# Dummy matmuls first, early zeroing on VectorE and an unheld w_in load in an attention-then-MLP kernel

## The chip, the cores and the metric

The kernel runs on one core of a Trainium2 chip. The metric is the device time of one execution in microseconds. Times of the kernel before are the median of three runs; the profile is of one further execution on the same core, taken by the hardware profiler.

## The reference

Batch 8, 8 heads, 576 positions, head dimension 64. First comes a Nyström form of attention with 32 landmarks: q and k are averaged over segments of 18 positions, three softmaxes are taken (q with the landmarks of k, landmarks with landmarks, landmarks of q with k), and the middle one is inverted by six Newton steps. The result goes through a two-layer MLP with squared ReLU.

```python
q_lm = q.reshape(B, H, m, S // m, D).mean(axis=3)
k_lm = k.reshape(B, H, m, S // m, D).mean(axis=3)
A = sm(q, k_lm)
Bm = sm(q_lm, k_lm)
C = sm(q_lm, k)
Z = Bm.transpose(0, 1, 3, 2) / (norm1(Bm) * norminf(Bm) + 1e-06)
for _ in range(6):
    Z = 2 * Z - Z @ Bm @ Z
x = A @ Z @ C @ v            # then heads side by side: 4608 x 512
r = np.maximum(x @ w_in, 0.0)
out = (r * r) @ w_out        # w_in 512 x 2048, w_out 2048 x 512
```

## The kernel before, in words

The eight batches are worked through one after the other. For a batch, the attention of batch b + 1 is woven into the MLP of batch b. The attention is folded into the first MLP matrix: instead of x the kernel forms G, a product of the small C times v with w_in, and multiplies it with the transposed rows of A (AT, or AZ with the inverse folded in, for batch 0). Function mlp_in does that for 16 feature tiles of 128 each (line 824), ScalarE takes the ReLU out of PSUM into a tile r (line 828), of which there are three, and VectorE squares it into gT (line 829). Function mlp_out multiplies gT with w_out (line 853).

The order of instructions on TensorE, VectorE, ScalarE and SyncE is written out by hand: the string HEAD holds the order for the attention of batch 0, and PLANS that of each batch after it, as tokens. In HEAD, ck casts k of batch 0 (VectorE one half at line 719, ScalarE the other at 720), tk and tq are TensorE transposes of k and q (line 315), tt those of the tail rows (line 325), mk and mq the segment means (line 344) with their evacuations at 359 and 360, ek, eq and et evacuations of transposes (lines 731 and 736), cq the copies of q (line 725), lm the landmark scores (line 374), ib, if, jo, jl and nu the inversion, and g the product with w_in (line 807). A token w:n:width issues n dummy matmuls of that width on zeros (function warm, line 297, 512 wide where no width is given); their result in the tile idle is never read. In PLANS, pk and pq prepare k and q of the next batch: a VectorE copy into another layout at line 283, from the tile stage for batches 1 and 2. Token h is one feature tile of mlp_in, s one squaring.

What isn't in that hand-written order is issued by a scheduler that goes by readiness: the constants at the start (zeroed tiles bd0, bd1, vt, ect, the segment matrix seg with GpSimd's band selections at line 206, the identity, the mask), and GpSimd's loads. GpSimd issues nearly all loads, one after the other, each held behind the one before by issue_after; k of batch 0 alone goes over the SyncE queue. The loads of batch 0's q come first. Function load_rest then queues the rest in the order of LOADS (two parts of w_in, v of batch 0, k and q of batch 1, two parts of w_in, four of w_out, v of batch 1). The first of these carries a further wait, called gate: it may not start before ScalarE's half of the cast of k is done. After the last of them GpSimd copies one column block of seg into the slot NC4 + 2, which the means of odd batches read at line 354, and zeroes two tiles ct0 and ct1 (line 264), 128 x 1280 bf16 each. These c-value tiles are read only where a batch number reaches DMA_C, which is 9.

```python
DMA_C = 9
        behind[:] = [masked]
        gate[:] = [after]
        for x in LOADS.split():
```

Of the kernel before, what the change touches and what calls it, by code (L numbers as in the profile page):

```python
# [9 lines left out]
P = 128  # L10
# [4 lines left out]
BF16 = mybir.dt.bfloat16  # L15
# [12 lines left out]
NC4 = 4  # L28
# [5 lines left out]
DMA_C = 9  # L34
COMPACT = 1
HEAD = (
    "ck tk1 mk w:1:256 w:1:256 ek1d w:1:256 w:1 tk0 tt w:1 w:1 cq0 cq1 ek0a mq tq0 tq1 lm "
    "w:1 et w:1:256 w:1 eq0a w:1:256 tl eq1d ls sum:0:4:5 w:1 ib w:1 w:1:256 sq1 w:1:256 if "
    "sk1 sum:1:2:5 w:1:256 w:1 sum:1:0:2 jo w:1:256 w:1:256 rec:1 w:1:256 row:1:0:3 "
    "row:1:3:5 w:1:256 sk0 w:1 sq0 jo w:1:256 w:1:256 w:1 w:1:256 sum:0:2:4 sum:0:0:2 w:1 jo "  # L40
    "rec:0 cv:0 cv:1 w:1:256 w:1:256 row:0:3:5 cr jo w:1:256 row:0:0:3 w:1:256 at:1 cba w:1 "
    "jl at:0 ea0d ea1a ct w:1:256 nu w:1:256 g:0 gl1d fv w:1 gf1d w:1 gf0a az gl0d"
# [46 lines left out]
def kernel(  # L89
# [9 lines left out]
    nc = tc.nc  # L99

    const = ctx.enter_context(tc.tile_pool(name="const", bufs=1))
# [19 lines left out]
    vts, ects, cts = [], [], []  # L121
# [8 lines left out]
    behind, gate = [], []  # L130

    def load(dst, src, queue=nc.gpsimd):
        with tc.issue_after(behind[0].ins) if behind else nullcontext():
            d = queue.dma_start(dst, src)  # L134
        if gate:
            tc.add_manual_dep(
                d.ins, gate.pop().ins.name,
                mybir.DependencyInfo(mybir.DependencyClass.Sync, mybir.DependencyReason.DATA),
                reason="q first")
        if queue is nc.gpsimd:  # L140
            behind[:] = [d]
        return d
# [66 lines left out]
    seg = const.tile([P, NC4 + 3, M], BF16, name="seg")  # L209
# [21 lines left out]

    EA = const.tile([P, 2, NC4 + 1, P], F32, name="EA")
    nc.vector.memset(EA[:, :, NC4, :], 1.0)

    def load_rest(after):

        def w_in(i, j):
            load(
                w_in_bf[64 * i:64 * i + 64, :, 1024 * j:1024 * j + 1024],
                moe_w_in[256 * i:256 * i + 256, 1024 * j:1024 * j + 1024].rearrange(  # L240
                    "(j d) f -> d j f", d=D),
            )

        def w_out(j):
            load(
                w_out_bf[:, 4 * j:4 * j + 4, :],
                moe_w_out[512 * j:512 * j + 512, :].rearrange("(ft fp) c -> fp ft c", fp=P),
            )

        behind[:] = [masked]  # L250
        gate[:] = [after]
        for x in LOADS.split():
            i = int(x[1])
            if x[0] == "w":
                w_in(i, int(x[2]))
            elif x[0] == "o":
                w_out(i)
            else:
                (load_v if x[0] == "v" else load_qk)(i, loaded[i])
        with tc.issue_after(behind[0].ins):  # L260
            nc.gpsimd.tensor_copy(seg[:, NC4 + 2, :], seg[:, NC4, :])
            for i in range(2):
                ct = const.tile([P, 2, NC4 + 1, P], BF16, name="ct%d" % i)
                nc.gpsimd.memset(ct[:], 0.0)
                cts.append(ct)

    turn = [0]

# [31 lines left out]
    def attention(b: int, R: dict):  # L300
# [410 lines left out]
        def head_step(token):  # L711
# [5 lines left out]
            if name == "ck":  # L717
                raw = natural(0, "k")
                dve(X["k"][:, 0:2], raw[:, 0:2])
                load_rest(act(X["k"][:, 2:4], raw[:, 2:4]))  # L720
                st["qraw"] = natural(0, "q")
                X["tT"] = attn.tile([P, NPAIR, P], BF16, tag="tT", name="tT")
# [253 lines left out]
```

The softmax here doesn't subtract the row's maximum and nothing guards it: scores larger than these inputs give would overflow.

## Time and profile before

| | us |
|---|---|
| median of three runs | 265.70 |
| the three runs | 265.61, 265.70, 266.66 |
| span of the profiled execution | 264.8 |
| TensorE busy | 248.2 |
| VectorE busy | 176.4 |
| ScalarE busy | 158.5 |
| GpSimd busy | 47.8 |
| first TensorE instruction starts | 8.01 |
| k of batch 0 cast by VectorE and ScalarE from | 6.91 |
| first w_in load issued | 8.25 |
| GpSimd's zeroing of ct0 and ct1 | 27.50, for 2.28 |

A group's line in the page gives the source line, engine, operation, the tile written and the tiles read, their shape and the count, then busy time and mean of one in ns. In the timeline the first two columns are start and length in microseconds, and a bracket holds the idle time of the engine before the instruction and what ended it. In the chain of waits each piece has its start, the time by which it alone moved the chain on, and its engine and line. PE is TensorE, PEld its weight loads, DVE is VectorE, ACT ScalarE and POOL GpSimd.

### The profile page before, as it was taken

What the parts mean: (1) busy time and instruction counts of PE and PEld (TensorE: products, weight loads), DVE (VectorE), ACT (ScalarE), POOL (GpSimd) and SP (SyncE); (2) the same over time, 40 slices, a digit from 0 to 9 for tenths busy, and PEclk for the clock granted to TensorE, in tenths of its full rate; (3) what the DMA queues carried; (4) which work ended last, traced back from release to release, by engine and by line L of the source; (5) the groups of instructions that cost most, each with busy time, mean ns of one, the idle gap of its engine ahead of it and who ended that gap; (6) DMA issues with size and microseconds to landing.
All of it is one profiled execution on the core that took longest, in us unless ns stands there. A gap on an engine that the chain in (4) does not pass through costs nothing.

```text
span 264.8 us, 6918 instructions
## 1 busy us (share of the span) xinstructions
PE 248.2 (94%) x2835; PEld 153.7 (58%) x2878; DVE 176.4 (67%) x485; ACT 158.5 (60%) x278; POOL 47.8 (18%) x73
## 2 busy tenths in 40 slices
PE   0799899999999999999999999999999999999994
PEld 0675665467665656566556565666566655555443
DVE  3488986879985779689766589689776884232100
ACT  1364887279666765678457565674777665365210
POOL 7744623302010500700003201320000000000000
PEclk9999999999999999999999999999999999999999
DMA  8999999998159899996829998999911111112122
GB/s 183 161 190 202 209 205 189 214 208 107 32 101 188 98 197 178 184 203 124 121 74 115 172 192 114 128 191 188 159 42 40 42 40 65 56 40 83 40 79 79
DMA packets 69791, 34.65 MB, mean 131 GB/s; under 512 B 37376, under 2 KB 64256, under 8 KB 69760
## 3 DMA queue, kind: packets, MB, share of 16 engines
q0 software_dynamic: 39808, 17.83, 54.2%
q1 hardware_dynamic: 24704, 7.08, 17.3%
q10 hardware_dynamic: 5248, 9.31, 11.3%
q8 instruction: 22, 0.36, 0.6%
q14 instruction: 9, 0.07, 0.1%
HBM read 36.70 MB, written 9.44 MB: 174 GB/s over the span
## 4 chain that ended last, share of the span: by engine, by line
PE 87%; DVE 5%; DMA 2%; issue 2%; ACT 2%; ACTq 0%
PE ops L853 24%; PE h L824 22%; PE n L853 21%; PE n L532 3%; PE g L807 3%; DMA stage<-in_k_dram 2%; PE idle L297 2%; PE n L416 2%; PE n L344 2%; PE n L598 2%; PE n L616 1%; DVE nat L283 1%; DVE gT L829 1%; PE tps L315 1%; PE n L631 1%
## 5 line engine op out<-in xcount | busy, mean ns | idle before, releaser
L828 ACT ACTIVATE r<-h 128x576 bf16<-128x576 f32 x128 | 81.3, 652 | 46.4 <-PE h L824 35.1
L853 PE MATMUL ops<-w_out_bf,gT 128*128 128x512 bf16 (+1 forms) x300 | 76.8, 368 | 0.9 <-issue 0.3
L853 PEld LDWEIGHTS <-gT 128*128 128x128 bf16 x592 | 53.2, 98 | 38.7 <-issue 4.2
L829 DVE TENSOR_TENSOR gT<-r 128x576 bf16<-128x576 bf16 x128 | 54.9, 448 | 26.3 <-ACT r L828 26.1
L824 PE MATMUL h<-AT,G 128*128 128x288 bf16 x448 | 71.0, 286 | 0.2
L853 PE MATMUL n<-w_out_bf,gT 128*128 128x512 bf16 x252 | 69.7, 379 | 1.1 <-issue 0.3
L824 PEld LDWEIGHTS <-G 128*128 128x128 bf16 x512 | 47.7, 97 | 24.3 <-issue 0.8
L705 DVE CAST G<-g 128x1024 bf16<-128x1024 f32 x14 | 17.1, 1224 | 5.4 <-PE g L807 5.4
L864 ACT COPY o_sb<-ops 128x512 f32<-128x512 f32 (+1 forms) x19 | 10.9, 574 | 14.5 <-PE ops L853 14.5
L864 ACT COPY o_sb<-n 128x512 f32<-128x512 f32 x17 | 10.0, 587 | 12.9 <-PE n L853 12.8
L705 ACT CAST G<-g 128x1024 bf16<-128x1024 f32 x14 | 14.2, 1013 | 4.5 <-PE g L807 4.5
L134 POOL DMA_DIRECT2D raw<-in_k_dram x5 | 4.6, 921 | 53.2 <-DVE gT L829 28.1
L532 PEld LDWEIGHTS <-T 128*128 128x128 bf16 x256 | 11.3, 98 | 4.2 <-issue 0.6
L574 DVE TENSOR_REDUCE ra<-EA 128x20 f32<-128x640 f32 (+3 forms) x19 | 13.2, 704 | 0.3 <-ACT EA L562 0.3
L586 DVE TENSOR_TENSOR an<-EA,rra 128x640 bf16<-128x640 f32 (+2 forms) x18 | 13.2, 736 | 0.2
L532 PE MATMUL n<-bd,T 128*128 128x64 bf16 x256 | 12.7, 193 | 0.3 <-issue 0.2
L315 PEld LDWEIGHTS <-nat 128*128 128x128 bf16 x96 | 6.8, 108 | 9.8 <-ACT nat L720 8.0
L537 ACT ACTIVATE EA<-n 128x512 f32<-128x512 f32 x16 | 9.6, 598 | 3.3 <-PE n L532 3.2
L134 POOL DMA_DIRECT2D raw<-in_q_dram x5 | 4.4, 884 | 38.5 <-DVE rc L447 28.1
L537 ACT ACTIVATE EC<-n 128x512 bf16<-128x512 f32 x16 | 9.5, 596 | 3.0 <-PE n L532 1.6
L315 PE MATMUL tps<-ident_bf,nat 128*128 128x128 bf16 x32 | 3.4, 278 | 8.0 <-ACT nat L720 8.0
L824 PE MATMUL h<-AZ,G 128*128 128x288 bf16 x64 | 10.0, 286 | 0.6 <-DVE AZ L797 0.4
(144 smaller groups left out, 294.6 us busy)
## 6 DMA issues: line engine op xcount, KB each, us to landing
out_dram<-o_sb ACTq DMA_DIRECT2D x31, 256.0 KB, 3.1
vm<-in_v_dram POOLq DMA_DIRECT2D x8, 512.0 KB, 10.1
raw<-in_k_dram POOLq DMA_DIRECT2D x5, 512.0 KB, 6.9
raw<-in_q_dram POOLq DMA_DIRECT2D x5, 512.0 KB, 6.1
w_in_bf<-in_moe_w_in_dram POOLq DMA_DIRECT2D x4, 512.0 KB, 12.1
w_out_bf<-in_moe_w_out_dram POOLq DMA_DIRECT2D x4, 512.0 KB, 17.2
out_dram<-o_sb ACTq DMA_DIRECT2D x9, 128.0 KB, 2.4
stage<-in_k_dram SPq DMA_DIRECT2D x1, 1024.0 KB, 6.1
```

Source lines behind the costliest of these rows:

```text
L134: d = queue.dma_start(dst, src)
L315: nc.tensor.transpose(tps[:, i, p, :], X[nm][:, 2 * half + i, 2 * p:2 * p + 2, :].rearrange("p h d -> p (h d)"), ident_bf[:],)
L532: nc.tensor.matmul(sc[:, c, j, :, :], lhsT=X[nm + "T"][:, c, p, :], rhs=BD[:, 1 if nm == "q" else 0, p, 0:64], start=True, stop=True)
L537: nc.scalar.activation(dst, sc.rearrange("p c j i m -> p c (j i m)"), AF.Exp, scale=SCALE)
L574: nc.vector.reduce_sum(ra[:, quads, lo:hi, :], EA[:, quads, lo:hi, :].rearrange("p q c (h m) -> p q c h m", m=M), axis=AX.X)
L586: on.tensor_tensor(an[:, i, lo:hi, :].rearrange("p c (h m) -> p c h m", m=M), EA[:, i, lo:hi, :].rearrange("p c (h m) -> p c h m", m=M), r ...
L705: (act, dve)[n % 2](G[:, :, n * 512:n * 512 + 512], gg[:])
L824: nc.tensor.matmul(h[:, j, 0:HALF], lhsT=G[:, qd, f * P:(f + 1) * P], rhs=AT[:, qd, a0 + j * HALF:a0 + (j + 1) * HALF], start=(qd == 0), s ...
L828: nc.scalar.activation(r.rearrange("p (j t) -> p j t", j=2), h[:, :, 0:HALF], AF.Relu)
L829: return lambda: nc.vector.tensor_tensor(gT[:, f, o:o + S], r[:], r[:], ALU.mult)
L853: nc.tensor.matmul(ops, lhsT=gT[:, f, t * P:t * P + P], rhs=w_out_bf[:, f, i * n:i * n + n], start=(f == 0), stop=(f == NF - 1))
L864: nc.scalar.copy(o_h, ops)
```

## The change

Three edits at the start of the kernel. HEAD begins with w:16, sixteen dummy matmuls 512 wide, ahead of the cast of k; they are meant to bring TensorE up to its full pace before real work arrives. The copy of the seg block and the zeroing of ct0 and ct1 move from GpSimd, behind its loads, to VectorE, next to the other constants. And the gate is gone: the first w_in load waits only until GpSimd has issued the mask, so that the loads behind it start earlier too.

```diff
 HEAD = (
-    "ck tk1 mk w:1:256 w:1:256 ek1d w:1:256 w:1 tk0 tt w:1 w:1 cq0 cq1 ek0a mq tq0 tq1 lm "
...
+    "w:16 ck tk1 mk w:1:256 w:1:256 ek1d w:1:256 w:1 tk0 tt w:1 w:1 cq0 cq1 ek0a mq tq0 tq1 "
...
     EA = const.tile([P, 2, NC4 + 1, P], F32, name="EA")
     nc.vector.memset(EA[:, :, NC4, :], 1.0)
+    for i in range(2):
+        ct = const.tile([P, 2, NC4 + 1, P], BF16, name="ct%d" % i)
+        nc.vector.memset(ct[:], 0.0)
+        cts.append(ct)
+    nc.vector.tensor_copy(seg[:, NC4 + 2, :], seg[:, NC4, :])
...
         behind[:] = [masked]
-        gate[:] = [after]
         for x in LOADS.split():
...
-        with tc.issue_after(behind[0].ins):
-            nc.gpsimd.tensor_copy(seg[:, NC4 + 2, :], seg[:, NC4, :])
-            for i in range(2):
-                ct = const.tile([P, 2, NC4 + 1, P], BF16, name="ct%d" % i)
-                nc.gpsimd.memset(ct[:], 0.0)
-                cts.append(ct)
```

The remaining lines of HEAD hold the same tokens, broken differently.

## The prediction

> **What bounds the kernel now.** I read the page's busy times, the chain of work that ended last, the timeline, and the traffic in half-microsecond stretches.
>
> ```profile
> PE 248.2 (94%) x2835; PEld 153.7 (58%) x2878; DVE 176.4 (67%) x485; ACT 158.5 (60%) x278; POOL 47.8 (18%) x73
> ```
>
> TensorE is busy 94% of the span, so from about 40 us on only less matmul work would help, and the change removes none there. What is left is the start: nothing runs on TensorE before 8.01 us, and a microsecond saved ahead of the steady part is a microsecond off the end, if nothing else holds the later work back. The chain of waits from 0 to 60 us begins so (start, length, piece):
>
> ```profile
> 0.81 6.08 DMA stage<-in_k_dram
> 6.91 1.05 ACT nat L720
> 8.01 1.03 PE tps L315 x8
> 9.04 0.53 PE n L344 x20
> 9.58 1.07 PE idle L297 x4
> 10.64 0.85 PE tps L315 x8
> 11.50 0.43 PE n L325 x4
> 11.92 0.85 PE idle L297 x2
> 12.78 0.53 PE n L344 x20
> 13.31 1.15 PE tps L315 x16
> ```
>
> The reader should see two things. Until 8.0 us the load of k and ScalarE's cast of it set the time. Then TensorE does, at half pace: two dummies 512 wide take 0.85 us, 0.425 each, and eight transposes take 0.85 to 1.03. Later in the same trace one 512-wide matmul of line 853 takes 0.22 in the chain, and eight transposes 0.45 (at 58.71). The sixteen at 13.31 take 1.15, between the two paces, so the switch came during them, near 13.7. The page's row for the granted clock reads 9 throughout and doesn't show it; the durations do.
>
> The second place is in batch 0's MLP (start, length, engine, line, tiles, and the idle time before with its releaser):
>
> ```profile
> 27.50 2.28 POOL L264 MEMSET ct<- 128x1280 bf16 x2
> 27.80 2.54 DVE L283 COPY nat<-stage 128x2048 bf16<-128x2048 bf16 x1
> 30.39 1.07 PE L315 MATMUL n<-ident_bf,nat 128*128 128x128 bf16 x16 [0.66 <-DVE nat L283]
> 30.79 1.19 ACT L828 ACTIVATE r<-h 128x576 bf16<-128x576 f32 x2 [0.90 <-DVE gT L829]
> ```
>
> The copy of q of batch 1 takes 2.54 us; the same copy of k at 26.21 takes 0.68. It ran beside GpSimd's two zeroings of the c-value tiles and ended 0.56 after them. TensorE and ScalarE then waited 0.66 and 0.90 for VectorE.
>
> The third is the load queue. Over these stretches the last column is GB/s:
>
> ```profile
> 8.50:9.00 0.50, 0.50 (x11) 0.50 (x9) 0.00 (x0) 0.00 (x0) 0.50 (x2) 1.00 1.35 183
> 9.00:9.50 0.50, 0.50 (x22) 0.50 (x20) 0.00 (x0) 0.00 (x0) 0.50 (x1) 1.00 0.47 59
> 9.50:10.00 0.50, 0.50 (x6) 0.31 (x3) 0.36 (x2) 0.32 (x2) 0.50 (x2) 1.00 1.03 61
> 10.00:10.50 0.50, 0.50 (x4) 0.21 (x2) 0.50 (x1) 0.21 (x1) 0.50 (x2) 1.00 0.52 49
> 10.50:11.00 0.50, 0.50 (x7) 0.50 (x6) 0.50 (x3) 0.00 (x0) 0.50 (x1) 1.00 0.84 160
> ```
>
> From 9.0 to 10.75 the loads nearly stop: batch 0's q is through, and the first w_in load was issued at 8.25, after 1.84 us of waiting for ScalarE's cast.
>
> [...]
>
> **The change, part by part.**
>
> *Sixteen dummies 512 wide, first in TensorE's order.* They need only bd1, zeroed by about 1.5. All slow, they take 16 x 0.425 = 6.8 us, to 8.4. [...] They lie beside the load of k; at worst they hold the first transposes by 0.4. Then the pieces above run fast. At half the time, eight transposes go from 1.03 to 0.52 and, at the 0.45 of 58.71, from 0.85 to 0.45, the dummies from 1.07 to 0.53 and 0.85 to 0.43, the tail's four transposes from 0.43 to 0.22, the sixteen from 1.15 to 0.90, the limit of the one row that has sixteen partly fast (at 0.056 each; both ends alike within 0.1). The two means (20 matmuls, 0.53) stay: 32 of them take 0.85 in full pace at 57.03, the same each. Sum before 6.44, after 4.11: 2.3 less. VectorE then has to follow: its evacuation (L360) at 9.06, the T copy until 10.08, the two casts of q (0.81) until 10.85, 0.2 after TensorE could take them. That leaves 2.1 in the profiled execution. q itself lands at 8.6 and 10.1 (issue 2.79 plus 5.8, and about 3.55 plus 6.5), before each cast needs it. From 14.6 on the work is fast already and only moves.
>
> The times before are 265.61, 265.70 and 266.66, and the profiled execution gave 266.55. [...] only the first pieces are slow: 0.51 + 0.54 + 0.40 less the 0.2, about 1.3. So 1.3 to 2.1; I take 1.5 for the median, which is near the low end of its three times.
>
> *Zeroing moves to VectorE, early.* Two of 128x640 uint32: from bd's 0.49 for 512, about 0.65 each, 1.3 together; as bf16 it would be 1.35 each, from seg's 224 in 0.245, so 2.7. VectorE is idle from 3.49 until k lands at 6.91 (3.42 us): both fit, with the copy of seg (under the 0.22 that blk's 128 columns take; GpSimd's last band on it is done by 5.8). So they cost nothing, hidden by the load of k. In exchange the q copy of batch 1 needs 0.68 and no 2.54. I followed it on: VectorE's first squares start at 28.5, not 30.26; ScalarE's fourth relu starts at 29.9, not 30.79; TensorE, which still has h and the transposes before it, resumes 0.65 earlier, and the means, the evacuations and the score matmul up to 34.7 follow by 0.6 to 0.7. Of the 1.86 that VectorE gains, 0.65 reaches the chain; the ends are 0.3 and 0.9 (ScalarE's wait). I take 0.65.
>
> *w_in's first load not held.* It issues once GpSimd's mask is done, near 6.4, 1.8 earlier, and every load behind it on the queue follows. The gap of 1.7 us at about 60 of 200 GB/s closes, so the queue runs ahead by about 1.2. Nothing waits for these loads now: batch 1's q lands at 26.4 (13.32 plus 13.1) for a copy at 27.80. With the head 1.3 to 2.1 faster that copy moves to 25.7 to 26.5, so without the earlier issue it would just begin to wait; with it, q is there by 25.2. The other loads have more room (first w_in pair by 20.4 for 23.43, w_out by 34.0 for 37.77). The part is worth nothing by itself and protects the first. New in its place: from 6.4 GpSimd writes descriptors while VectorE casts k (6.91)[...]. VectorE's copies of q at 10.55 ran beside such descriptor work in 0.42 and 0.48, against 0.34 for half of the large copy's 0.68, so about 0.1 longer; tk0 has more slack than that.
>
> Sum: 1.5 + 0.65 = 2.15, 265.7 - 2.15 = 263.55, say 263.5. Both parts shift later work unchanged, as loads from batch 3 on are released by VectorE's work.
>
> **The rivals.** *The shift is smaller (16%).* The scheduler may put the zeroings behind the cast of k on VectorE, since line 224 already stands there, and L360 then comes at 8.9 to 10.3; or loads bind again at 26 us. The first costs up to 1.2 of the head: 0.3 + 0.65, 264.7. For it speaks line 224's place; against it, that line 224 waited for a mask and the memsets wait for nothing. *The head gains all of it (20%).* 2.1 + 0.9 = 3.0: 262.7. For it: the profiled execution. *Slower (5%).* If VectorE's cast of k were locked out through the whole run of descriptor work from 6.4, it would start near 12.4 rather than 6.91, with the means after it at 13.1 instead of 9.04; less the 2.1 and 0.65 that is some 1.3 later, 267.0. The copies at 10.55, which got in between, speak against it, and the 2.54 at 27.80, which did not get in between two memsets, for it.
>
> **How the numbers follow.** Likeliest (59%): 263.5. The range from 262.5 to 264.8 takes in the full gain and the small one and leaves out the slower case, and tails of the rest. Faster by over 0.5% means under 264.4: the likeliest and the full case, 79%, and of the small one a little: 0.80. Within 0.5%: 0.14. Slower: 0.06.
>
> **What would show it.** Right: sixteen dummies from about 1.6 to 7 or 8; eight transposes at 8.0 in about 0.5 us; the score matmul of line 374 near 12.3 rather than 14.3; the q copy of batch 1 at 0.68 and ScalarE's 0.90 gone; w_in issued near 6.4 with no dip at 9 to 10.5. Wrong: transposes at 8.0 still at 1 us, TensorE waiting longer for VectorE or for q at 10 to 11, a long cast of k, or a wait of the q copy for its load.

## The result and the profile after

The changed kernel takes 263.34 us (median of four, 263.24 to 263.84) against 266.0 before: ratio 0.9901, 95% interval 0.9875 to 0.9927. Forecast were 263.5, in a range of 262.5 to 264.8, and faster. A ratio here and below is close to that of two means: the executions of one version against those of the kernel before that ran beside it. A time beside a ratio is a median.

The dummies, the zeroings, the first w_in load and batch 1's q copy in the timeline of the kernel after (start, length, engine, line, tiles; line numbers are two or so lower than before):

```profile
1.52 5.33 PE L295 MATMUL idle<-bd 128*128 128x512 bf16 x16 [1.52 <-DVE bd L117]
3.57 1.27 DVE L236 MEMSET ct<- 128x640 uint32 x2
6.37 0.65 POOL L134 DMA_DIRECT2D w_in_bf<-in_moe_w_in_dram  x1
...
25.63 0.68 DVE L281 COPY nat<-stage 128x2048 bf16<-128x2048 bf16 x1
```

The dummies end at 6.85, before k is cast. The zeroings were turned into 640 uint32 each, as each of the bd tiles had been into 512 before (0.49 on the mean), and are over at 4.84, with VectorE idle until 6.72. The copy of the seg block didn't go into that gap: it ran behind the cast of k, at 7.42. The load is issued 1.88 earlier, and from 9.0 to 10.5 the loads move 205 to 235 GB/s in each half microsecond, where they moved 49 to 61 before. The q copy takes 0.68, not 2.54. The chain of the kernel after, up to the landmark scores (start, length, piece):

```profile
0.81 5.89 DMA stage<-in_k_dram
6.72 1.05 ACT nat L718
7.82 0.62 PE tps L313 x8
8.44 0.51 PE n L342 x20
8.97 0.29 DVE bd L358
9.30 0.69 DVE T L729
9.99 0.93 DVE nat L723 x2
10.97 0.41 PE n L342 x10
11.38 0.90 PE tps L313 x16
12.28 0.09 PE n L372 x4
```

The first eight transposes fell from 1.03 to 0.62, and from 8.97 to 10.92 VectorE carries the chain, not TensorE. To see where the 2.7 us between the two profiled spans (264.8 and 262.1) come from, I set the starts of all 128 ReLUs of ScalarE side by side. The lead of the changed kernel is 2.17 us at the first, 3.18 from the fourth on, 3.16 for a hundred microseconds and more, and 2.72 from the 85th (173.8 us before, 171.05 after) to the last. So there are three steps: 2.17 in the head, 1.01 at the q copy, and 0.44 given back late. Of the 2.17, 0.19 is k landing earlier in that execution (ScalarE's cast starts at 6.72, not 6.91); from that cast to the score matmul it is 5.40 instead of 7.38, which leaves 1.98 for the pace of TensorE. I call this stretch, from the cast to the score matmul, the head time below.

Of the late loss, 0.34 is one small VectorE instruction on the chain at batch 6's inversion, 128 x 2 elements in 0.51 where the same one took 0.17 before (columns as in the timeline; the first two lines are after, the last is before):

```profile
168.34 0.91 POOL L134 DMA_DIRECT2D vm<-in_v_dram  x1
168.73 0.51 DVE L442 TENSOR_SCALAR c<-n 128x2 f32<-128x2 f32 x1
...
171.80 0.17 DVE L444 TENSOR_SCALAR c<-n 128x2 f32<-128x2 f32 x1
```

In the kernel after it lies beside GpSimd's descriptor work for a load. From the tenth ReLU to the last, the fourteen profiles of this study lie between 208.1 and 208.5; before has the least of them and the changed kernel the most, and 208.41 when run again, so I count this as variation of single executions and not as an effect of the change.

### The profile page after: what moved, and what is told of

It is laid out like the page before. It is cut to its first block, busy times and chain, and to the rows that moved or that the text cites. A ratio compares the mean times of both kernels' runs of the same rounds, so it can differ in the third digit from the quotient of the medians.

```text
span 262.1 us, 6993 instructions
## 1 busy us (share of the span) xinstructions
PE 254.6 (97%) x2894; PEld 154.1 (59%) x2894; DVE 176.8 (67%) x488; ACT 158.4 (60%) x278; POOL 45.2 (17%) x70
## 4 chain that ended last, share of the span: by engine, by line
PE 91%; DVE 4%; DMA 2%; ACT 1%; issue 1%; DVEq 0%
PE ops L851 25%; PE h L822 24%; PE n L851 22%; PE g L805 3%; PE n L530 3%; DMA stage<-in_k_dram 2%; PE n L342 2%; PE n L414 2%; PE n L596 2%; PE idle L295 2%; PE n L614 1%; PE n L313 1%; PE n L629 1%; ACT r L826 1%; PE n L558 1%; DVE gT L827 1%
## 5 line engine op out<-in xcount | busy, mean ns | idle before, releaser
L851 PE MATMUL ops<-w_out_bf,gT 128*128 128x512 bf16 (+1 forms) x320 | 81.7, 368 | 0.0
L851 PE MATMUL n<-w_out_bf,gT 128*128 128x512 bf16 x272 | 74.5, 379 | 0.0
L862 ACT COPY o_sb<-ops 128x512 f32<-128x512 f32 (+1 forms) x19 | 10.9, 574 | 14.5 <-PE ops L851 14.5
L295 PE MATMUL idle<-bd 128*128 128x512 bf16 (+1 forms) x51 | 13.3, 377 | 1.5 <-DVE bd L117 1.5
L414 PEld LDWEIGHTS <-ED 128*128 128x128 bf16 x72 | 6.8, 98 | 6.5 <-DVE EY L453 0.9
```

The source lines that it names most:

```text
L295: nc.tensor.matmul(idle[:, 0:width], lhsT=z[:, 0:P], rhs=z[:, 0:width], start=True, stop=True)
L414: nc.tensor.matmul(res[a:a + w, qd, :], lhsT=diagonal[a:a + w, qd, :], rhs=moving(qd)[a:a + w], start=True, stop=True)
L851: nc.tensor.matmul(ops, lhsT=gT[:, f, t * P:t * P + P], rhs=w_out_bf[:, f, i * n:i * n + n], start=(f == 0), stop=(f == NF - 1))
L862: nc.scalar.copy(o_h, ops)
```

## The experiments

The first four runs apply one of the three edits, or leave one out, to see which of them carry the gain.

**Dummies alone.**

```diff
-    "ck tk1 mk w:1:256 ...
+    "w:16 ck tk1 mk w:1:256 ...
```

> The kernel before with the sixteen dummy matmuls alone. Theory (three separate effects: pace of TensorE 1.3 to 2.1 us, the zeroings beside the q copy of batch 1 about 1 us, the load queue only as protection): eight transposes near 8 us take 0.6 instead of 1.03, score matmul of line 374 near 12.4, and the time falls by 1.3 to 2.2 us, to 263.8 to 264.7. But q of batch 1 lands near 26.4 as before while its copy is now due at 25.7, so the copy should show a wait of about 0.7 for its load. Rival (the earlier loads carry the gain): TensorE's faster start is used up waiting for q or w_in, and the time falls by under 0.5 us.

Ratio 0.9921 (0.9890 to 0.9952), 263.64, so the rival falls. Head time 5.66. By the ratio the gain is 2.1, inside the expectation, but it didn't come from the head alone. What I had not expected is in batch 0's MLP (timeline of this run):

```profile
25.69 0.69 DVE L283 COPY nat<-stage 128x2048 bf16<-128x2048 bf16 x1
...
26.80 2.28 POOL L264 MEMSET ct<- 128x1280 bf16 x2
```

The zeroings are still on GpSimd, still behind its loads, but the faster head brings VectorE's copy there 1.1 us ahead of them, and it takes 0.69. So in this execution the dummies alone avoid the collision, and the fourth ReLU follows the first by 3.40, much as in the changed kernel (3.41), not by 4.42. One of the six executions took 264.87, the others at most 263.90; whether the copy met the zeroings there was not profiled. The forecast wait for q's load is at most 0.07 here. The chain shows a cost of the dummies as well:

```profile
1.53 6.49 PE idle L297 x16
8.02 0.45 PE tps L315 x8
```

In this execution the pace rose later (the dummies' weight loads still start 0.42 to 0.43 apart up to 7.05, and 0.37 for the next) and the dummies lasted until 8.02, though k had been cast by 7.43: the transposes start at 7.85 in the timeline, 0.4 after they could have.

**Zeroing on VectorE alone** (the hunk of the change that moves the seg copy and both memsets).

> The kernel before with the zeroings and the seg copy moved to VectorE alone. Theory: the q copy of batch 1 takes 0.68 instead of 2.54, the head is unchanged, and the time falls by about 1.0 us, to about 265.0 (ScalarE's wait of 0.9 and what TensorE lost). Rival (VectorE's other work absorbs it, or the zeroings delay the cast of k): under 0.3 us, or the first TensorE instruction later than 8.0.

Ratio 0.9962 (0.9947 to 0.9976), 265.04: 1.0 us, as expected. One of its 22 executions took 647.65 us; it is not in the ratio, and why it did is not known. The copy takes 0.68, and the fourth ReLU follows the first by 3.41. The memsets cost nothing: k's cast starts at 6.75, 0.02 after k has landed.

**Gate away alone.**

```diff
         behind[:] = [masked]
-        gate[:] = [after]
```

> The kernel before with the gate on the first w_in load taken away alone. Theory: w_in is issued near 6.4, the dip in traffic at 9 to 10.5 us closes, k and q of batch 1 land 1.2 to 1.8 us earlier, but nothing waited for them: within 0.3 us of before. It may even lose some 0.3 where descriptor work slows VectorE's casts. Rival (the earlier loads carry the gain): faster by 1 us or more.

Ratio 1.0019 (0.9995 to 1.0043), 265.64 where the kernel before had 266.14: no gain of 1 us or more, so the rival theory falls. But "within 0.3 of before" isn't the whole of it. Of the 22 executions thirteen took 264.87 to 265.95 and nine 266.75 to 268.60. The profiled one, 267.4, is of the slower nine, and its trace shows what can be lost:

```profile
25.60 2.28 POOL L263 MEMSET ct<- 128x1280 bf16 x2
25.88 2.55 DVE L282 COPY nat<-stage 128x2048 bf16<-128x2048 bf16 x1
```

Earlier loads bring GpSimd to its zeroings at 25.60 rather than 27.50, and they now meet the copy of k of batch 1 instead of that of q. Here the fourth ReLU follows the first by 5.24 rather than 4.42. The means of the two groups lie 2.4 apart, the ReLUs of the profiled one show 1.8 of it as this collision's cost (5.24 less 3.41). That the other thirteen missed it is likely, but none of them was profiled.

**Gate put back** (dummies and zeroing on VectorE).

> The changed kernel with the gate put back (dummies and zeroing on VectorE, first w_in load held until ScalarE's cast of k is done). Theory: the head keeps its 2.1 us, but the q copy of batch 1, due at 25.6, waits for its load until about 26.2, so the part that the gate removal protects shows as 0.3 to 0.8 us: 263.6 to 264.1 where the changed kernel has 263.3. Rival (the gate is worth nothing): the same time as the changed kernel within 0.2.

Ratio 0.9915 (0.9889 to 0.9941), 263.65: not told apart from the changed kernel, so neither the 0.3 to 0.8 of the theory nor the 0.2 of its rival is settled. The wait that the gate removal was to prevent is there:

```profile
25.95 0.69 DVE L282 COPY nat<-stage 128x2048 bf16<-128x2048 bf16 x1 [0.40 <-DMA stage<-in_q_dram]
```

But the fourth ReLU still follows the first by 3.40. The copy ends at 26.64, and TensorE reaches the transposes that read it only at 27.23, after other work.

**Zeroing left on GpSimd** (dummies, no gate).

> The changed kernel with the zeroings left on GpSimd behind its loads. Theory (a collision decided by phase): without the gate GpSimd reaches the zeroings near 25.5, and with the fast head VectorE is due at one of its two 2048-wide copies (24.0 and 25.6) just then, so one copy takes 2.5 instead of 0.68 or the two just miss each other; in the first case the gain after the head falls from 1.0 to about 0 and the time is 264.3 to 265.0. Rival (moving the zeroings is worth nothing, as dummies alone reach the changed kernel's time): 263.3 to 263.7, and both copies at 0.68.

Ratio 0.9936 (0.9911 to 0.9960), 264.34. The fifteen executions lie in two groups, seven from 262.96 to 263.79 and eight from 264.34 to 264.93, with means 1.5 apart; the two collisions profiled before cost 1.0 (before) and 1.8 (gate away alone) by the ReLUs. The profiled one (263.34) is of the first, with a near miss:

```profile
25.27 0.68 DVE L282 COPY nat<-stage 128x2048 bf16<-128x2048 bf16 x1
26.35 2.28 POOL L263 MEMSET ct<- 128x1280 bf16 x2
```

That the second group are the hits is an inference; none of it was profiled. The spread itself, here and with the gate away alone, says that without the gate and with the zeroings left on GpSimd the time depends on the execution.

**Eight dummies in place of sixteen.**

```diff
-    "w:16 ck tk1 mk ...
+    "w:8 ck tk1 mk ...
```

> The changed kernel with eight dummies in place of sixteen; they end near 4.9 us, 3.4 us after their start. Theory [...] the first transposes near 7.8 are slow again, and the time is 1 to 2 us above the changed kernel, 264.3 to 265.4. Rival (any early matmul is enough to raise the pace): 263.3, with transposes at 7.8 in 0.6.

Ratio 0.9972 (0.9953 to 0.9991), 264.86, inside the expectation. Head time 6.51, with transposes at 1.03 again. The stretches of this run (length, busy time of PE with its count, then the other engines; the third column from the right is the granted clock):

```profile
1.50:4.20 2.70, 2.67 (x7) 1.02 (x8) 2.56 (x12) 0.58 (x1) 2.70 (x4) 1.00 0.72 192
4.30:7.70 3.40, 0.48 (x3) 0.01 (x1) 1.61 (x5) 1.04 (x1) 3.28 (x13) 1.00 1.55 256
7.75:11.10 3.35, 3.35 (x42) 2.89 (x43) 1.78 (x5) 0.52 (x2) 3.35 (x6) 0.50 1.28 207
11.20:13.60 2.40, 2.40 (x49) 2.03 (x48) 1.08 (x4) 1.48 (x4) 2.21 (x3) 1.00 1.37 194
```

The eight were over at 4.78. At half pace they would have lasted until about 5.1 (an estimate from starts 0.42 apart and 0.63 for the last, as for the two at 11.72 in the trace before), so the pace had risen by then. But k's transposes, which begin at 7.69, after TensorE had been idle for 2.92 us, take 1.03, and the half pace lasts until about 11.1: at 11.18 the tail's four transposes take 0.26 in the chain, and at 11.44 two wide dummies 0.43. So in this execution the slow transposes came as I expected, although the clock had been up before them, and the rival was wrong. The column of the granted clock reads 0.50 only in the third stretch; in the first it reads 1.00, though seven dummies fill 2.67 us there, at half pace. What sets the moment of a rise or a fall was not shown. In the six profiles with sixteen that show it the dummies end between 6.59 and 8.02 and leave TensorE idle for at most 1.12 us, about 1 in the changed kernel, and in all eight k's first eight transposes take 0.45 to 0.62: there the clock holds. How long an idle time it bears was not tried between 1.12 and 2.92.

**Half and double the zeroing on GpSimd**, from the kernel before. In the first, one of the two tiles (never read in this configuration) isn't zeroed at all.

```diff
-                nc.gpsimd.memset(ct[:], 0.0)
+                if i == 0:                      # half
+                    nc.gpsimd.memset(ct[:], 0.0)
...
+                for _ in range(2):              # double
+                    nc.gpsimd.memset(ct[:], 0.0)
```

> The kernel before with one of the two c-value tiles zeroed by GpSimd and the other not at all (it is never read). Theory (VectorE's large copy is shut out until GpSimd's zeroings beside it are through): the copy that meets it takes about 1.35 in place of 2.54, less by one zeroing of 1.18, and ScalarE's wait of 0.9 before its fourth relu goes down to nothing. Rival (the copy is slow for another reason, such as loads into the same memory): still about 2.5.

One profile, 265.16:

```profile
26.94 1.18 POOL L265 MEMSET ct<- 128x1280 bf16 x1
27.15 1.51 DVE L284 COPY nat<-stage 128x2048 bf16<-128x2048 bf16 x1
```

The copy ends 0.54 after the zeroing, as before's ended 0.56 after both: in these two executions VectorE was held until GpSimd was through. The fourth ReLU follows the first by 3.41, so a copy lengthened by 0.83 costs nothing, while one lengthened by 1.86 costs 1.01: some 0.85 of it is slack.

> The kernel before with each c-value tile zeroed twice by GpSimd. Theory: the copy that meets them takes 2.54 plus 2 x 1.18 = 4.9, if it is shut out for the whole row of them, and the end comes about 2.4 later than before (268.1) since everything after it waits. Rival: it gets in between two zeroings, under 3 us.

One profile, 265.83, and not the test I meant:

```profile
26.87 2.58 DVE L284 COPY nat<-stage 128x2048 bf16<-128x2048 bf16 x1
27.09 2.41 POOL L261 COPY seg<-seg 128x32 bf16<-128x32 bf16 x1
29.45 4.47 POOL L265 MEMSET ct<- 128x1280 bf16 x4
```

VectorE's copy had started before GpSimd's small seg copy. Both then took about 2.5, the small one in place of 0.22, and the four zeroings came after. The 4.9 that I expected could not show, and why two copies hold each other up for some 1.9 us is open. The fourth ReLU follows the first by 4.48, so meeting the small seg copy cost as much as meeting the zeroings. The change takes that copy from GpSimd too, and no run moved the one without the other.

**A version meant to beat both.** VectorE carries the chain at 9 to 10.9, so its first copy of q was moved ahead of the evacuation of k's means.

```diff
-    "w:16 ck tk1 mk ... w:1 w:1 cq0 cq1 ek0a ...
+    "w:16 ck tk1 cq0 mk ... w:1 w:1 cq1 ek0a ...
```

> The changed kernel with VectorE's first copy of q moved ahead of the evacuation of k's means. In the changed kernel VectorE carries the chain from 8.97 to 10.92. q's first half lands near 8.5 and VectorE is free from 8.3 to 9.0. Theory: the second means of q start 0.4 earlier, and the time falls by 0.3 to 0.5 below the changed kernel, to about 262.9. Rival (q's second half, landing near 10.1, or TensorE bounds here): within 0.1 of 263.3.

Ratio 0.9915 (0.9882 to 0.9948), 263.52: no gain. Three small constant copies of VectorE, whose order is not written by hand, slipped in behind the moved copy and held the evacuation until 9.39. Head time 5.44.

> The same move of q's first copy, with the gate kept (dummies, zeroing on VectorE, first w_in load held). Theory: with the gate there is no descriptor work beside VectorE's copies of q before 8.2, so they take 0.8 together and not 1.0; the head is as fast as in the version without the gate or 0.1 to 0.2 faster, and the q copy of batch 1 waits for its load by up to 0.8, which ScalarE's slack there takes up in part: 262.8 to 263.4. Rival (the earlier loads now count): at least 0.3 slower than the same move without the gate.

Ratio 0.9934 (0.9910 to 0.9959), 264.0, head time 5.66: the expectation failed. The time is 0.5 above that of the same move without the gate, as the rival had it, though the intervals of the two ratios overlap. The two profiles differ in the head (5.66 against 5.44) and after it: here batch 1's q copy waits 0.57 for its load, and the fourth ReLU follows the first by 3.58, not 3.41. The copies of q took 0.51 and 0.55 with the gate too: q's first half landed just ahead of 8.31, and GpSimd was writing descriptors from 7.95.

Next the three small copies went to GpSimd, ahead of its loads:

```diff
-    nc.vector.tensor_copy(blk[:], mask4[:, :].unsqueeze(2).to_broadcast([P, 4, M]))
+    nc.gpsimd.tensor_copy(blk[:], mask4[:, :].unsqueeze(2).to_broadcast([P, 4, M]))
...
-        behind[:] = [masked]
+        behind[:] = [placed]      # the last of the three copies
```

> The changed kernel with VectorE's first copy of q moved ahead of the evacuation of k's means, and the three small constant copies that stood in the way (two of blk, one of seg) given to GpSimd ahead of its loads. In the run with the move alone they filled 8.7 to 9.4 and held the evacuation back by 0.4. Theory: q's first copy runs at 8.4 to 8.8, the evacuation at 8.9, and the second means of q end 0.4 earlier: 262.9 where the changed kernel has 263.3. Rival (q's second half, landing near 10, or the copies on GpSimd beside the cast of k take it back): within 0.15 of the changed kernel.

Ratio 0.9923 (0.9896 to 0.9951), 263.8:

```profile
8.24 0.90 POOL L134 DMA_DIRECT2D vm<-in_v_dram  x1
8.49 0.91 DVE L724 COPY nat<-stage 128x1024 bf16<-128x1024 bf16 x1 [1.14 <-DMA stage<-in_q_dram]
```

The moved copy takes 0.91 beside the descriptor work for v, where in the first of these three versions it took 0.43 (beside that for the tail of v), so the evacuation starts at 9.43, as late as before the three copies were moved. Head time 5.34.

> The changed kernel once more, for comparison on the same chip and with the same runs of the kernel before: 263.2 to 263.9.

Ratio 0.9919 (0.9886 to 0.9952), 263.46, head time 5.31. No version tried is told apart from the changed kernel on the better side. The changed kernel's eleven executions lie between 263.13 and 263.95. The 96 of the kernel before that ran beside the experiments go from 264.04 to 267.13, so the change also takes away most of the spread. Two things vary in the traces, when the pace rises and whether a VectorE copy meets GpSimd; how much of the spread each makes was not measured.

| head time, from ScalarE's cast of k to the score matmul, one profile each | us |
|---|---|
| before; gate away; half zeroing | 7.38; 7.50; 7.29 |
| double zeroing; eight dummies; zeroing alone | 6.74; 6.51; 6.48 |
| all with sixteen dummies | 5.31 to 5.66 |

The second row has no lasting early pace either, but there the rise came sooner after the work began: in the chain of the run with the zeroing alone the two wide dummies at 11.57 take 0.43, where the same pair took 0.85 before. From these single profiles the head gain is about 0.8 to 2.2 (an estimate), depending on where the rise falls.

## Why the prediction was right

- **TensorE's half pace in the head** was named rightly. Forecast were 2.1 for the profiled execution and 1.5 for the median; the profile gives 1.98. Over the executions it was less: with the zeroings already moved, adding the dummies takes the ratio from 0.9962 to 0.9915, about 1.3 us, the low end of the forecast 1.3 to 2.1. The 1.3 supposes an execution whose pace rises sooner, so that only the first pieces are slow; that was an estimate, and the trace before does not show one. The run with the zeroing alone does: its pace is up at 11.57. The dummies were to end at 7 or 8, or at 8.4 if all were slow: they ended at 6.85 and, in the six profiles with sixteen that show it, between 6.59 and 8.02. Where they ended at 8.02 they held the transposes by the 0.4 forecast as the worst.
- **The hand-over to VectorE** at 9 to 10.9 came as forecast, except that the two copies of q took 1.00 in the timeline and not 0.81, beside descriptor work. The score matmul was forecast near 12.3 and came at 12.12 with k 0.19 early. A slip of the prediction did no harm: it has batch 0's q through at 9.0 in one place and its second half landing at 10.1 in another; in the trace of the kernel before it lands at 10.0.
- **The zeroings on VectorE** were forecast at 1.3 together, hidden: 1.27, hidden. The copy of seg, forecast in the same gap at under 0.22, ran behind the cast of k and took 0.53, at no visible cost: VectorE's next work on the chain had to wait for TensorE anyway.
- **The q copy** is the term that was mis-sized: I took 0.65 for what reaches the chain. It is 1.01, in the changed kernel and with the zeroing moved alone. The step that was off is the one by which TensorE "resumes 0.65 earlier": its first feature tile after the sixteen transposes starts at 28.33 against 31.49 before, which is 0.99 earlier once the 2.17 of the head is taken off. From 24.90 to 29.53 its pieces follow one another in the chain without a gap.
- **The sum** comes out, and partly by luck. Counted one after the other, the zeroings are worth 1.0 and the dummies on top of them about 1.3, together 2.3 with the gate kept (ratio 0.9915). The copy was forecast too low (0.65) and the head a little too high (1.5), so 2.15 came near. The changed kernel gained 2.6 in the first comparison and 2.2 when run again. What the prediction did not see is that the two edits, each taken alone, share a gain: the dummies alone are worth 2.1, since they also move the copy out of the zeroings' way, as in the one profile of that run, and 2.1 and 1.0 do not make 3.1.
- **The gate's removal** was rightly worth nothing alone. As protection, it spares a wait of 0.40 that no later work felt; with q's first copy moved ahead the wait was 0.57, and 0.17 of it may have been felt. What I had missed is the other direction: it can pull GpSimd's zeroings forward onto VectorE's copies, as in the profile of the gate away alone, so the zeroings should move with it.
- **The rivals.** The smaller gain and the slower case did not come: VectorE's cast of k took 0.78 beside descriptor work instead of 0.69, and 0.69 beside it with q's first copy moved ahead, so it was not shut out. In the profiled execution the full gain of the rival "all of it" was there until 168 us, 3.2, and ended at 2.7.

## What to carry to other kernels

Find the pace of TensorE from the time per matmul of the same shape early and late, since the row of the granted clock can read full where the durations say half (before it reads 9, its top digit, throughout, with 0.425 and 0.22 for 512 columns); if matmuls run at half pace while other engines wait, fill the idle time before them with dummies that last until shortly before the real work (here the pace held over 1.12 us without a matmul and was lost over 2.92); an overrun delays it (0.4 us in one run here). Look for single instructions far over the median of their group, and for what GpSimd did in that stretch. Two edits that both remove the same collision do not add up, so measure each alone and all but one. Look at all the times of a version and not only at the median: two groups of times point to something that happens in some executions and not in others.

## What the runs showed that I had not expected

- Raising the clock isn't enough: after eight dummies and 2.92 us without a matmul the head ran at half pace again from 7.69 us to 11.1.
- In three profiles GpSimd's zeroings held VectorE's copy until the last was done: with two it took 2.54 and 2.55 and ended 0.56 and 0.55 after them, with one 1.51 and 0.54. It didn't get in between the two.
- Beside GpSimd's writing of descriptors VectorE's copies between SBUF tiles took longer, but not each time: 0.43 or 0.91 for 1024 columns, and a copy of 128 columns took 0.53 at 7.49 in the changed kernel and 0.22 at 7.43 with the zeroing alone, where no descriptors were written just then.
- A GpSimd copy of 32 columns and a VectorE copy of 2048 that overlapped took 2.41 and 2.58, against 0.22 and 0.68 apart. Not explained here.
